# The first group of queries in two parts: an early bound over one key chunk, and sums rescaled afterwards

## The chip, the cores and the metric

The kernel runs on one core of one Trainium2 chip. Five engines work from instruction queues of their own: TensorE (PE, matmuls), VectorE (DVE), ScalarE (ACT, activation functions), GpSimd (POOL) and SyncE (SP, which here only issues DMAs). They meet at semaphores. The metric is the device time of one execution in microseconds, as the median of repeated runs; lower is better.

## The reference

Input x has 2048 tokens of 640 bf16 features. A layer norm gives xn. Two branches read xn, and the output joins them:

```python
x = A_x
xn = _layernorm(x, axis=-1)
s = _A_ref(xn, A_wqkv, A_wo)                       # attention, 32 heads of 20 features
g = _silu(_B_ref(xn, B_w1, B_w2, B_w3, B_w4))      # gated MLP: norm, w1, gelu, shifts, w2, residual, norm, w3, gelu, w4, residual
return x + s * g
```

In the attention, `scores = q @ k.T * Dh**-0.5`, `p = softmax(scores)` over all 2048 keys, `o = p @ v`, and o is projected by wo. 32 heads of 2048 x 2048 scores are 134 million exponentials, which makes the softmax the largest piece of work outside PE.

## The kernel before

**Tiles.** Tokens come in 16 tiles of 128 and 4 chunks of 512. The heads are worked four at a time ("quads", 8 of them), each head on 32 partitions (20 features and a 21st row for the bound). A *group* is one quad and one chunk of 512 queries: 32 groups, named quad_chunk (0_0, 0_1 and so on). For a group and a key tile, a score pair (`score_pair`, two heads, 128 keys x 512 queries each) goes to two PSUM banks; `exp_act` lets ACT take exp of 1024 values per partition into SBUF (line 1604), or, for some tiles named in `BLK` and `UNITS` ("units"), DVE forms the exponential's bits (line 1635, named u...) and pieces of it are shifted by DVE or POOL (lines 1524 and 1522, named s...). `fnpv` (line 1358, named pv...) and line 1536 (named pvd...) multiply by the values and add up in one PSUM bank, PVB. The value matrix has a column of ones, so the sums of the softmax come out with the products. `normalise` transposes the bank (line 1656, named ob...), and divides.

**The bound.** exp needs a shift that is at least roughly the largest score. The kernel takes an upper bound: for each query the sum over features of |q| times the largest |k| of this feature over all keys. In `prep`, `mx_c` reduces |K| of key chunk c (line 1152), `kev_c` copies the keys out on ACT (line 1155, after `mx_c`), `mx_` and `mq_` (lines 1167, 1169) combine the four chunks. `aq_c` takes |q| (line 1129), `sh_c` multiplies it by the bound (four matmuls, line 1136) and `qad_c` adds the result to the queries as their 21st row (line 1142). So no score of group 0_0 can be formed before the keys of all four chunks are projected.

**The opening.** x is loaded in eight DMAs of two tiles (`ld_x0` to `ld_x14`), the weights of the first quad in `ld_wp_1` (keys), `ld_wp_0` (queries), `ld_wv0` (values). The first layer norm is done per tile on DVE (`ln_tiles`: statistics at line 913, norm at line 942, or on POOL at line 938 for tiles in `POOLN`; the power -1/2 on POOL) or on ACT (`ln_tiles_act`: two passes with an accumulator, lines 959 and 961, norm at line 997, or on POOL at line 993). Chunks 0, 1 and 3 are transposed on PE (line 1050, named tr_x) and copied out by ACT (line 1058) or DVE (line 1061), named trev_x; the four tiles of chunk 2 by DMA transposes from SP (tx_8 to tx_11, line 1039). `query(c)`, the key projections KT_c and the value projections v0_n (copied out by vev0_n, line 1296) follow, all through `mm_tile` (line 703). PE also has 36 dummy tasks (`warm`, line 876).

**What sets the order.** The program makes a list of tasks, each with its engine, reads and writes. `TABLE` is a string that lists all of them in one global order, two characters each, with a character for each PSUM or buffer slot; `follow` reads it. Each engine issues its tasks in that order and waits at a task until its operands are there. Nothing is reordered at run time. POOL's tasks and the tasks marked `lock` on DVE are kept apart by waits that `follow` adds.

**Later work.** Groups 0_1 onward need `QM`, a buffer with each head's queries alone on its 32 partitions; POOL zeroes it once (`qm0`, line 1172), and SP copies the queries in (`qm0_1` and so on). The keys and queries of the other quads are projected in "stacks" (s1_0_c is the first, line 1234 copies it out) after SP has loaded `ld_ws0_1`. The MLP branch starts with the loads `ld_w1` and `ld_w2`.

Of the kernel before, what the change touches and what calls it, by code (L numbers as in the profile page):

```python
# [472 lines left out]
class Cfg:  # L473
# [5 lines left out]
    def __init__(self, S=2048, D=640, H=32, F=1536):  # L479
# [20 lines left out]
        self.POOLN = [2, 4, 7, 15]  # L500
# [17 lines left out]
        self.VP0 = False  # L518
# [18 lines left out]
        self.LNA = [3, 2]  # L537
# [36 lines left out]
        self.HP = True  # L574
        self.PP |= {(quad, qc, 0, 2) for quad in range(8) for qc in range(4)}


    def order(self, quad, qc):

        nb = self.ND[quad][qc] % 10
        used = [k for b in self.BLK[:nb] for k in b]
        ks = [k for k in range(self.NT) if k not in used]
        at = {}
        for j, (pos, r, n) in enumerate(self.UNITS[self.ND[quad][qc]]):
            at.setdefault(pos, []).append(("b", j, r, n))
        rows = self.NR[quad][qc]
        out = []
        for i in range(len(ks) + 1):  # L590
            out += at.pop(i, [])
            if i < len(ks):
                out.append(("r" if i in rows else "w" if 100 + i in rows else "k", ks[i]))
        assert not at
        return out
# [22 lines left out]
def c_act(n):  # L618
    return 68 + 0.8333 * n
# [13 lines left out]
class Gen:  # L633
# [149 lines left out]
    def setup_consts(self):  # L783
# [35 lines left out]
        self.free("ones_bf", "ones_f", "m1", "e4", "maskn6")  # L819
# [60 lines left out]
    def xlat(self, n):  # L880
        return 500.0 if n in (2, 4) else 1300.0
# [140 lines left out]
    def ln1_and_transpose(self):  # L1022
# [5 lines left out]
        for g0 in range(0, NT, 8):  # L1028
            na = cfg.LNA[g0 // 8]
            for k0, L in ((0, 2), (2, 2), (4, 4 - na))[:3 if na < 4 else 2]:  # L1030
                tl = list(range(g0 + k0, g0 + k0 + L))
                tmp += self.ln_tiles(f"ln1_{g0 + k0}", tl, lambda n: xn[:, n, :], lambda n: [A("xn", n)], ve_out=True)
            tmp += self.ln_tiles_act(f"ln1a_{g0}", list(range(g0 + 8 - na, g0 + 8)))
# [42 lines left out]
    def prep(self):  # L1076
# [69 lines left out]
        query(0)  # L1146
        for c in range(NQC):
            at = [A("KT", 0, c)]
# [23 lines left out]
        T("pool", 3840, lambda e: e.memset(self.QM[:, :, :, :], 0.0), reads=after, writes=[A("QM", k) for k in range(2)], name="qm0", due=self.at(8))  # L1172
# [4 lines left out]
        shift(0)  # L1177
        for c in range(1, NQC):
            query(c)
            shift(c)  # L1180
# [128 lines left out]
    def attn_quad(self, quad):  # L1309
# [9 lines left out]
        for qc in range(NQC):  # L1319
# [15 lines left out]
            def ends(done=done, total=total):  # L1335
                done[0] += 1
                return done[0] == 1, done[0] == total
            for kind, x, *unit in seq:
                if kind == "k":
# [203 lines left out]
    def score(self, e, out, b, qc, kt, i):  # L1543
        return e.matmul(out, self.KT[32 * i:32 * i + 32, b, 128 * kt:128 * kt + 128], self.QT[32 * i:32 * i + 32, b, 512 * qc:512 * qc + 512],  # L1544
                        start=True, stop=True, tile_position=(32 * i, 0))

    def score_pair(self, b, qc, kt, a, hs, sa, gb):
        T, A = self.T, self.A
        me = []
        def fn(e):  # L1550
            for jj in range(2):
                out = self.bank(hs[jj].slot if isinstance(hs, tuple) else hs.slots[jj])
                if me[0].mode:
                    ins = self.score(e, out[:, :], b, qc, kt, 2 * a + jj)
                    continue
                for c in range(4):
# [4 lines left out]
                    reads=[A("KT", b, kt // 4), A("QT", b, qc), A("QTa", b, qc)] + ([] if gb is None else [A("QM", gb)]),  # L1561
# [80 lines left out]
    def normalise(self, quad, qc):  # L1642
# [9 lines left out]
        else:  # L1652
# [3 lines left out]
        T("dve", c_dve(512), lambda e: e.transpose(Ob[:, :], self.bank(self.PVB)[:, :]),  # L1656
          writes=[("PV", 0), A("Ob")], name=f"ob{quad}_{qc}", cls=cls)
# [191 lines left out]
    def b_alloc1(self):  # L1849
# [9 lines left out]
        vea = [A("VE", n) for g0 in (0, 8) for n in sorted({g0, g0 + 2, g0 + 4, g0 + 8 - cfg.LNA[g0 // 8]})]  # L1859
# [193 lines left out]
    r"#a#9#t$G#,#%#&$R###'7,#8$<#$$$#6$,#:#*#+#;#(#)&J&K$%#-#0#i#.#<$&$'#=#>#`#x#u$($)#v#y#?#w#z$*#@#b#{#_#m#|#j#A#B$-$+#C#D#k#E#n#F$.$/$0%(&#l#G$1#H%-'#I#o"  # L2053
    r"#J#}#K#p#L$3#M#N#d$I#O$K$L#P#f$_$H#q$M$J#h#~#Q$2#R#r$z#$u$#s%#%$p($`%$$q&I$4$5${$|$v$#$k)$l$m$r$w$x$6$N$O#g#c$=#e$>$7$}$s$a$~$?#S$b$n$o$Q$8$;$y$A%D$@$"
    r"B%%$P%&#T%'$C$D$S#U#V$W#W#X$c$E$e#Y#Z#[$t%_#%C%`$d#]$9%f$%g%.$:$F$f%a%b%c&L%%d%2(%/%0%3%4%5%)%*%<)%h$T%i%6$V$U&M$^%+$g$X$Y%1%7#%8$Z%,&b(%=&c%9&N%:&d%;"
    r"%>%?%@&S'%j%k$h&T&U&V$]&O%m#%l&P&e%n$[&W%o%p&f%T$%q%J&%E)&X&Q&g%K$i%L%Y'%Z$j%[%U%]%^%F%G%M%V%N%H%I%O%%P%Q%R%A%S%W%X%B%t(%u%v%r%w%x%{$%y%|%}%e%s%~%z&#&"
    r"$&.%&&&/&'&0&1&7#&8&%&,&&9&:&2#2&-&;&3)~#*$'*#$*+(17*%&4*,)*'#*-$*.(*)*&(&<*(#*6#*2$*3$#^*8&5#*/*0(*1)*5#*7%&=&Z(&[&]'[&^&_&6&o#&p&q&r&(&s&)*P(&`&h*Q&"
    r"*:$*9#&t*4&@#&A*;)*<&B&C*K(*L$*I$&D&E**&i&&j&k&>'&?&l&m*N'*J#&|$&}&~&n*^$*O'*_('#'$*M*U#'%*S'*R*T#&u$&v&w*?&x&y&z''('(')(@'*+%,2(A'+*h&*e(*V$*>*H*f&*i"
    r")'A&'B'C'D'E',*W*Z%*j(*A&F'F'3#'4'&'5'6&G&&H*[#'7'8&{*`$*=*o##5*E*k$*c(*l*a%'-#'.'/'0'1*p''2':(';'<'='>*t#*b'?+'&+)*d)*m('M('@*u$'N'O'P'Q'R*n%*X#'9*Y("
    r"*g++&+-*y(*z&'G('H'I*G+&#'J'K'L*w&+()+5(+7*]'T(*x#'U'V+H#+I('W'X#4*B+J(+9&&a*q'S+K''Y+;'Z*F*{+*#'^('_+S&*r(+U*D+,#*@+^#'`*s%*C*v*|+/&+_&+1(+2$'a(?'b'c"  # L2060
    r"'d&'e'f+.+W(+Y+8%+0%'g(B+:)'h'i+R&+T#+3+4%+[(+<+6$+L'j#'k'l'm+a#+D+V$'n+]'+E+X%+>'p$+`&+'q'r#7+b&,#$,$('o+g''s*}+i't+='u'v+c#+d'+k$']+|'+Z(C(E$+z#+m+e"
    r"+A(F+C,4$+}#(D(G(J,<'+?+{%+F,=&,(#,)'+B+G+o+M'(<+O#,6+N)+P$,8$+~+n+@+j'+l#'w,:'y$(`'z+v,%#'{'|+Q,*$+f'+x.H+s+u'}+t,&%,'+p,3#,+),B$+h$'~+w+r,,,5%-=18,E"
    r"'(#$($,D,F$,]#,G),^(,H+q*~+#+y,-,7',9#(%(&,A$,>#,?$('((,I,C'(H,J()#(*(+,a(,Z#,c,@(,(-&*,k$,;(.,[$,e(,l&,W#,_,X#(/#(0,g,d$(1,f$(2(3,i#(Q,j(,n(,o%,T,Q,K"
    r"(n(R((S(T(U,U#,V)(4(5(=,t&(V,m,p(,M,S,x#,N,v-c&(W,L,Y,z,q&,`((K((L-d',b),|,},w#,s&,u#(M,y((N(O(P,r,P#/,O-+&(o((p,h-,%+$(u'x-$(q(8-.#(r-/),R(6(s,{(t-*-"
    r"?(-3&-4#-0#-%-A(7((9-1$-5&-C(-#-6(,.(g---B#-D%-E-2,~(:(;->&-M(-&-',/,0-@)-O-(-I#,1-)-7-G(-8-J$.](-H#.^-9-Q&-S-P#._.`.a-h(.b-F-L&-R&.J&&Y-i(.K-a%-l(.L-"
    r"N)-b%.M.N-V.P#.Q-`.O(>.R-f$-g)-v#.S-n-w&(I.T-K.U-T.V$.W-o$.6'.7#.X.Y.Z.[-q$-e-p#-k'-m%-U(v$(w-r-j-t$-y#-u(-z)-]-_(x(y(z-Y.8'.'$-W.9'-^-x-{#-s.d-X-Z.e-"
    r"|(-~'.).#$({.I.&#(Y$.c(Z.$$.(%-[.%./.>'-}([.?&.,.:.;$(](^)<(X.f#.g.h(_.i&R.j.*.k.@(.<'.A)2H2R#2J$2L.=.0.l#...m2S#3[2X(2T$2Z2U'.n.o.p2N#2P.22M$2O(.5.4."
    r"B-:-;.32[(2]#2^)2W$.q.-.r#.s2_.1.+.C2I(2Y$2n#.t.u.v.x(2o%2k.y)C2s#2b.D.z2K&.{.|.w2w(3#&2t)2d2V2v#.}.~(h(3$$(i2Q3%&2y2{(2x#(j3,#(k(l2}2`3&'3(&3.&3)(3'3"
    r"*(2c3<#(m)6(3=$3+2e2g3-&2h2z(3;2|'2f2q#)7)83/)92r&2l(323C&(|2i2m(2j2~2u35):3D#2a3>#3?)38)5);3K(312p3F&-<.E3M3H'.F(}((~.G36333A#3G(3J&)`4g3I)#3B%)$)%)&"
    r")J303L&3@3^#3`3](3_)344%&4&$(a((b3:3h(3i(3b#373E3O3f&3d393U3l(3g#4##3Q3N)'(c3a&4$%3c&3P3S3T3n3R3k#3m'3p(41&3V3j3r43#4'/#(d(e/%3o#3q$4((3t4)%)=#)>)?)@)"  # L2070
# [106 lines left out]
```

## Time and profile before

| | |
|---|---|
| median of 3 runs | 806.92 us (805.21 to 808.1) |
| profiled execution, first to last instruction (span) | 799.9 us; the page has no other time for it |
| median run less this span | 7.0 us |
| mean granted TensorE clock | 0.998 |
| busy: PE / ACT / DVE / POOL | 768.0 / 765.4 / 688.9 / 438.8 us |
| first exponential of group 0_0 starts on ACT | 29.84 us |
| the last of the key chunks is copied out by ACT from | 27.66 us |
| first KT/QT matmul on PE | 15.93 us |

Times are from the first instruction of the profiled execution. "Busy" counts the time in which an engine executes; in a timeline a bracket gives the idle time just before the instructions of a line and what released them. Instructions of an engine overlap a little, so the mean length of one (1041 ns for a 1024-wide exponential) is more than the distance between two (40 of them in 36.88 us, 0.92 each).

### The profile page before, as it was taken

The page shows a single profiled execution, that of the slowest core. Times are in us where ns is not written, and L with a number is a line of the kernel's source. Part 1 is how long each engine was busy: PE and PEld are TensorE (multiplying, and loading weights), DVE is VectorE, ACT ScalarE, POOL GpSimd, SP SyncE. Part 2 cuts the span into 40 slices and gives each one's busy share as a digit, 9 for nine tenths or more (in the row PEclk, how much of TensorE's full clock was granted, in tenths as well). Part 3 has the DMA queues.
Part 4 walks back from the last instruction along what each step waited for, and adds up shares of the span by engine and source line. Part 5 has one row for each costly group of instructions (what it writes and reads, how often), then busy time and mean ns, then how long its engine had stood idle before and what let it go on. Part 6 is the DMA issues. An engine that isn't in the chain of part 4 may idle for free.

```text
span 799.9 us, 29391 instructions
## 1 busy us (share of the span) xinstructions
PE 768.0 (96%) x13308; PEld 316.8 (40%) x13308; DVE 688.9 (86%) x908; ACT 765.4 (96%) x797; POOL 438.8 (55%) x232
## 2 busy tenths in 40 slices
PE   7899999999999999999999999999999999998996
PEld 3443333334444433333434444334333444443463
DVE  7868889989999999899988889898878888787767
ACT  7799999999999999999999999999999999999994
POOL 5466556452546647666644655755344454745742
PEclk9999999999999999999999999999999999999999
DMA  6202653243241322524232132314322213115252
GB/s 180 31 14 68 150 145 87 55 117 55 37 86 34 48 68 57 86 54 78 77 100 53 19 82 53 84 36 71 75 63 71 45 37 82 19 28 152 78 151 84
DMA packets 141356, 58.20 MB, mean 73 GB/s; under 512 B 113728, under 2 KB 136432, under 8 KB 141232
## 3 DMA queue, kind: packets, MB, share of 16 engines
q1 hardware_dynamic: 141232, 56.33, 30.9%
q8 instruction: 104, 1.70, 0.9%
q14 instruction: 20, 0.16, 0.1%
HBM read 34.70 MB, written 10.33 MB: 56 GB/s over the span
## 4 chain that ended last, share of the span: by engine, by line
ACT 60%; PE 34%; DVE 4%; DMA 2%; issue 0%; SPq 0%; DVEq 0%
ACT arena L1604 54%; PE psum L703 12%; PE psum L1544 8%; PE psum L1536 5%; PE psum L1358 3%; PE psum L1557 3%; DVE arena L1635 2%; ACT arena L1586 2%; ACT arena L2009 1%; ACT arena L1917 1%; ACT arena L2037 1%; DMA arena<-in_A_x_dram 1%; PE psum L1415 1%; PE psum L1419 1%; DMA arena<-in_B_w_dram 0%; DMA arena<-arena 0%
## 5 line engine op out<-in xcount | busy, mean ns | idle before, releaser
L1604 ACT ACTIVATE arena<-psum 128x1024 bf16<-128x1024 f32 x726 | 677.0, 1041 | 16.1 <-PE psum L1544 11.6
L1522 POOL TENSOR_TENSOR arena<-arena 128x2048 int32<-128x2048 int32 x92 | 330.5, 3600 | 212.2 <-DVE arena L1524 98.7
L1635 DVE TENSOR_SCALAR arena<-psum 128x1024 uint16<-128x1024 f32 x268 | 325.6, 1218 | 51.9 <-PE psum L1544 46.4
L703 PE MATMUL psum<-arena 128*32 128x320 bf16 (+1 forms) x5808 | 329.5, 332 | 2.0 <-DMA arena<-in_B_w_dram 0.7
L1544 PE MATMUL psum<-arena 32*128 32x512 bf16 x1634 | 195.1, 384 | 14.7 <-ACT arena L1604 8.8
L703 PEld LDWEIGHTS psum<-arena 128*32 128x32 bf16 x5808 | 140.9, 96 | 120.8 <-issue 28.8
L1536 PE MATMUL psum<-arena 128*22 128x512 bf16 x2144 | 184.7, 381 | 2.2 <-DVE arena L1524 1.1
L1358 PE MATMUL psum<-arena 128*22 128x512 bf16 x1448 | 137.4, 381 | 0.2
L1524 DVE TENSOR_SCALAR arena<-arena 128x4096 uint16<-128x4096 uint16 (+1 forms) x127 | 133.6, 1075 | 3.4 <-PE psum L1536 2.5
L1544 PEld LDWEIGHTS psum<-arena 32*128 32x128 bf16 x1634 | 53.9, 91 | 183.0 <-ACT arena L1604 101.9
L1557 PE MATMUL psum<-arena 128*32 128x512 bf16 x1400 | 106.7, 381 | 0.1
L1536 PEld LDWEIGHTS psum<-arena 128*22 128x22 bf16 x2144 | 51.3, 91 | 66.8 <-issue 29.9
L1664 POOL TENSOR_TENSOR arena<-arena 128x512 bf16<-128x512 f32 x30 | 41.1, 1369 | 42.3 <-DVE arena L1524 22.3
L1358 PEld LDWEIGHTS psum<-arena 128*22 128x22 bf16 x1448 | 35.6, 91 | 44.3 <-issue 18.9
L1557 PEld LDWEIGHTS psum<-arena 128*32 128x32 bf16 x1400 | 28.5, 95 | 38.8 <-ACT arena L1604 28.7
L2002 DVE CAST arena<-psum 128x512 bf16<-128x512 f32 x48 | 32.8, 684 | 8.0 <-PE psum L703 7.8
L1234 DVE CAST arena<-psum 128x512 bf16<-128x512 f32 x40 | 26.9, 682 | 5.5 <-PE psum L703 5.5
L913 DVE BATCH_NORM_STATS2 arena<-arena 128x6 f32<-128x320 bf16 x54 | 24.6, 481 | 2.8 <-DMA arena<-in_A_x_dram 2.7
L1586 ACT ACTIVATE arena<-psum 128x2048 bf16<-128x2048 f32 x13 | 24.6, 1891 | 1.9 <-PE psum L1544 1.8
L1763 DVE SCALAR_TENSOR_TENSOR arena<-psum,arena 128x320 bf16<-128x320 f32 x32 | 15.4, 486 | 12.4 <-PE psum L703 12.0
L1656 DVE STREAM_TRANSPOSE arena<-psum 128x512 f32<-128x512 f32 x31 | 22.1, 711 | 3.4 <-PE psum L1536 1.6
L1825 POOL TENSOR_TENSOR arena<-arena 128x640 bf16<-128x640 bf16 x12 | 16.8, 1400 | 13.1 <-DMA out_dram<-arena 4.7
(122 smaller groups left out, 335.5 us busy)
## 6 DMA issues: line engine op xcount, KB each, us to landing
arena<-in_B_w_dram SPq DMA_DIRECT2D x48, 160.0 KB, 2.7
arena<-arena SPq DMA_DIRECT2D x124, 32.0 KB, 1.9
arena<-in_B_w_dram SPq DMA_DIRECT2D x4, 960.0 KB, 5.6
arena<-in_A_x_dram SPq DMA_DIRECT2D x8, 320.0 KB, 5.5
arena<-in_A_x_dram SPq DMA_DIRECT2D x16, 160.0 KB, 2.9
out_dram<-arena SPq DMA_DIRECT2D x16, 160.0 KB, 2.3
heads<-arena SPq DMA_DIRECT2D x120, 20.0 KB, 2.0
arena<-keys SPq DMA_DIRECT2D x28, 80.0 KB
```

What stands on the lines that cost most here:

```text
L703: ins = e.matmul(pb[32 * c:32 * c + 32, 0:N], lhsT(k, c), rhs(k, c), start=(k == 0), stop=(stop and k == nk - 1), tile_position=(0, 32 * c))
L1358: ins = e.matmul(pb[32 * i:32 * i + 22, 0:512], VA[:, ql, kts[i // 2], i, :], PT[:, slots[i // 2][0].slot, 512 * (i % 2):512 * (i % 2) + 512],
L1522: return e.tensor_tensor(dst.bitcast(I32), U[:, ub, 0:w].bitcast(I32), bass.AP(c.tensor, c.offset, [list(c.ap[0]), [0, w // 2]]), op=ALU.add)
L1524: fa if onp else lambda e, v=v, dst=dst: e.tensor_scalar(dst, U[:, ub, 0:w], EXP_B[v], None, op0=ALU.add),
L1536: ins = e.matmul(pb[32 * i:32 * i + 22, 0:512], wv, dst[:, at:at + 512].bitcast(BF16), start=first, stop=final, tile_position=(0, 32 * i))
L1544: return e.matmul(out, self.KT[32 * i:32 * i + 32, b, 128 * kt:128 * kt + 128], self.QT[32 * i:32 * i + 32, b, 512 * qc:512 * qc + 512], s ...
L1557: ins = e.matmul(out[32 * c:32 * c + 32, :], self.KT[:, b, 128 * kt + 32 * c:128 * kt + 32 * c + 32], self.QM[:, gb, 2 * a + jj, :], start ...
L1586: lambda e: e.activation(self.PT[:, hp[0].slot:hp[0].slot + 2, :], self.psum[:, 512 * h0.slot:512 * h0.slot + 2048].rearrange("p (a b) -> ...
L1604: lambda e: e.activation(self.PT[:, hp.slot, :], self.psum[:, 512 * hs.slot:512 * hs.slot + 1024], AF.Exp, scale=cfg.scale),
L1635: ins = e.tensor_scalar(U[:, ub, 1024 * at + 512 * k:1024 * at + 512 * k + w], self.psum[:, 512 * hd.slots[k]:512 * hd.slots[k] + w], a_ex ...
L1664: return e.tensor_tensor(OnT.rearrange("p (k d a) -> p a k d", k=4, a=4), Ob[:, :].rearrange("p (a k d) -> p a k d", a=4, k=4), in1, op=AL ...
L2002: T("dve", c_dve(512), lambda e, h=h, fc=fc, i=i, G=G: e.tensor_copy(G[:, i, fc, :], self.wbank(h)[:, 0:512]), reads=[wa], writes=at, name ...
```

## The change

Group 0_0 takes its first four key tiles (0 to 3, key chunk 0; `EARLY = 4`) with other queries than the rest. `early` makes a bound from chunk 0's keys alone (`mqe` from `MXc[0]`, `she` on PE) and adds it to the queries in a buffer of its own (`qade`, into `QE`, which lies in the room of `QM`). Scores of tiles 0 to 3 use `QE`, and their products add up in PVB. When the bound over all keys is known (`qad_0`, as before), `between` forms the difference of the two bounds for every query and head (`fs`: 8 matmuls with the selection matrices `sel`) and ACT takes its exponential (`fe`). `rescale` on DVE multiplies the sums of the first part by it into `Ob`; the bank starts afresh for the other 12 tiles; `sum0_0` adds both parts, and the transpose follows. All four early tiles go through ACT; the group's two units are the key blocks (6, 7) and (10, 11), where they were (2, 3) and (6, 7). `qm0` is moved behind `rescale`, since `QM` holds the early buffers.

```diff
-        self.POOLN = [2, 4, 7, 15]
+        self.POOLN = [6, 8, 9, 14, 15]
-        self.VP0 = False
+        self.VP0 = True
-        self.LNA = [3, 2]
+        self.LNV = [[0], [2, 3], [6, 7], [8, 9], [10, 11], [12, 13]]
+        self.LNS = [[1], [4, 5], [14, 15]]
+        self.EARLY = 4
+        self.PP |= {(0, 0, 1, 3), (0, 0, 1, 2)}
...
+        first = 0 if quad + qc else 1
+        used = [k for b in self.BLK[first:first + nb] for k in b]
...
+            at.setdefault(pos, []).append(("b", j + first, r, n))
...
+        at = at if quad + qc else {k + self.EARLY: v for k, v in at.items()}
...
+        QE = self.QM.rearrange("p a i q -> p (a i q)")
+        self.qe, self.fe = QE[:, 0:512], QE[:, 512:1536].bitcast(FP32)
+        mqe = QE[:, 1536:1664].rearrange("p (j m) -> p j m", m=32)
+        sel = QE[:, 1664:1920].rearrange("p (s j m) -> p s j m", s=2, m=32)
+        def early():
...
+            T("dve", 90, lambda e: e.tensor_scalar(mqe[:, :, 20], self.maskn[:, 0:4], MXc[:, 0:1], None, op0=ALU.mult),
+              reads=[A("MXc", 0), A("maskn"), A("mqe")], writes=[A("mqe")], name="mqe", lock=True)
...
+                for j in range(4):
+                    ins = e.matmul(pb[32 * j:32 * j + 32, 0:512], mqe[:, j, :], self.KS[:, 0:512], start=True, stop=True, tile_position=(0, 32 * j))
...
+            T("dve", c_dve(512),
+              lambda e: e.scalar_tensor_tensor(self.qe, self.wbank(h)[:, 0:512], self.qbias[:, 0:1], QT[:, 0, 0:512], op0=ALU.add, op1=ALU.add),
+              reads=[wa, A("qbias"), A("QT", 0, 0), A("QTa", 0, 0)], writes=[A("QE")], name="qade", rel=h)
+        def between():
...
+                for k in range(2):
+                    for j in range(4):
+                        ins = e.matmul(pb[32 * j:32 * j + 32, 0:512], sel[:, k, j, :], QT[:, 0, 0:512] if k else self.qe, start=k == 0, stop=k == 1,
+                                       tile_position=(0, 32 * j))
...
+            T("act", c_act(512), lambda e: e.activation(self.fe, self.wbank(h)[:, 0:512], AF.Exp, scale=cfg.scale), reads=[wa], writes=[A("FE")],
+              name="fe", rel=h)
         for c in range(NQC):
+            if c == 1:
+                early()
...
-        T("pool", 3840, lambda e: e.memset(self.QM[:, :, :, :], 0.0), reads=after, writes=[A("QM", k) for k in range(2)], name="qm0", due=self.at(8))
...
         shift(0)
+        between()
...
+                if kind == "f":
+                    T("dve", c_dve(512), lambda e: e.tensor_tensor(self.Ob[:, :], self.bank(PVB)[:, :], self.fe, op=ALU.mult), reads=[A("FE")],
+                      writes=[("PV", 0), A("Ob")], name="rescale", cls=-1)
+                    T("pool", 3840, lambda e: e.memset(self.QM[:, :, :, :], 0.0), name="qm0",
+                      writes=[A("QM", k) for k in range(2)] + [A("QE"), A("FE"), A("mqe"), A("sel", 0), A("sel", 1)])
+                    continue
...
+            T("dve", c_dve(512), lambda e: e.tensor_tensor(both, self.bank(self.PVB)[:, :], Ob[:, :], op=ALU.add), reads=[A("Ob")],
+              writes=[("PV", 0), A("On", 0), A("On", 1)], name="sum0_0", cls=cls)
```

The order table is another one throughout. Read off by task names, the opening changes as follows (sx and sxx are the two ACT statistics of a tile, exp a_b with a the key tile and b the pair of heads, shortened):

```
ACT before: sx5 sxx5 sx6 sxx6 sx7 sx14 sxx7 sxx14 sx15 sxx15 trev_x0 x3, norm5 norm6 qev_0 trev_x1 x5, kev_0 norm14
            trev_x3_3 kev_1 kev_2 kev_3 | exp 2_0 0_0 0_1 3_1 1_1 1_0 6_0 ...
ACT after:  sx1 sxx1 sx4 sxx4 norm1 sx5 trev_x0_1 sxx5 trev_x0_4 sx14 trev_x0_2 sxx14 norm5 norm4 kev_0 qev_0 trev_x1 x5,
            sx15 sxx15 | exp 2_1 0_0 1_1 kev_1 exp 2_0 3_0 trev_x3_3 exp 1_0 3_1 kev_2 kev_3 exp 0_1 | 6_0 5_0 fe ...
SP before:  x4 x2 x6 x0 x10 x14 wp_0 wv0 wp_1 x8 x12 | tx_11 tx_10 tx_8 tx_9 ld_ws0_1 qm0_1 qm0_2 ...
SP after:   x0 x2 x4 x6 x8 wp_1 x14 x10 x12 wv0 wp_0 | tx_9 ld_w1 tx_8 tx_10 tx_11 qm0_1 ld_ws0_1 ld_w2 qm0_2 ...
DVE after, from mx_0 on: mx_0 norm7 mqe nb8 (12: rest of the statistics of tiles 10, 11, 13, 12, aq_0 among them) vev0_0 vev0_2 qade
            vev0_1 vev0_3 norm10 norm12 norm11 vev0_7 mx_1 vev0_5 norm13 vev0_6 qev_1 rve, trev_x3 x4, mx_2 ve2 mx_3 mx_ mq_
            vev0_10 aq_1 qad_0 qev_3 u 6 qev_2 u 7 rescale ...
POOL after: ... norm6, norm9, norm8, norm14, norm15, ... r2 qm0 vp0_10 kt0 s0_0_1_3 ... s0_0_1_2 ...
PE after, around the first scores: KT_1 ... sc 2_1 0_0 ... KT_2 ... KT_3, v0_10, sc 0_1 sh_0 ... sc 6_0 ... fs pv k1 ... pv k3 v0_12 ... pv b1
```

Behind the opening, ACT's order is the same from about its 65th to its 270th task but for single exchanges; after that many short stretches differ on all engines.

## The prediction

> **What bounds the kernel now.** First view, busy times and shares of the whole span:
>
> ```profile
> PE 768.0 (96%) x13308; PEld 316.8 (40%) x13308; DVE 688.9 (86%) x908; ACT 765.4 (96%) x797; POOL 438.8 (55%) x232
> ```
>
> ACT and PE are both full to 96%, so I asked where their few idle us lie. Busy time by stretch (columns: stretch and length, then busy us of PE, PEld, DVE, ACT, POOL, then clock, DMA share, GB/s):
>
> ```profile
> 0.00:30.00 30.00, 23.75 (x588) 12.74 (x588) 24.09 (x85) 20.36 (x39) 14.77 (x39) 1.00 0.59 139
> 30.00:60.00 30.00, 28.63 (x500) 12.81 (x500) 22.13 (x34) 29.72 (x33) 17.88 (x16) 1.00 0.05 11
> 60.00:100.00 40.00, 38.77 (x594) 13.43 (x590) 33.73 (x39) 39.63 (x43) 24.90 (x14) 1.00 0.45 109
> 100.00:300.00 200.00, 198.32 (x3322) 79.94 (x3320) 185.00 (x235) 194.06 (x197) 106.08 (x44) 1.00 0.33 73
> 300.00:780.00 480.00, 465.85 (x8008) 190.65 (x8010) 409.14 (x492) 472.09 (x480) 269.77 (x119) 1.00 0.30 69
> ```
>
> ACT idles 9.64 us in the first 30, then 0.28 and 0.37 up to 100. From 100 to 300 PE is the fuller one (1.7 idle in 200), after 300 ACT again (7.9 idle in 480). A lead won on both engines before 37 us therefore has hardly a gap to disappear into. Third view, the chain that ended last, in order of time (start, length, what):
>
> ```profile
> 18.63 2.14 ACT arena L1058 x5
> 20.76 3.69 DMA arena<-arena
> 24.55 3.64 PE psum L703 x64
> 28.60 0.75 DVE arena L1142
> 29.35 0.66 DVE arena L1127
> ```
>
> The chain runs through the DMA transposes of token chunk 2 (they land at 24.46), the key projections of chunks 2 and 3, and qad_0 (28.60), which puts the bound over all keys into the queries. Only then comes the first exponential. ACT's timeline from there back, with the idle time in brackets:
>
> ```profile
> 24.16 0.60 ACT L1058 ACTIVATE arena<-psum 128x512 bf16<-128x512 bf16 x1 [1.27 <-PE psum L1050]
> 25.61 0.78 ACT L1155 ACTIVATE arena<-psum,arena 128x512 bf16<-128x512 f32 x1 [0.86 <-DVE arena L1152]
> 26.59 0.78 ACT L1155 ACTIVATE arena<-psum,arena 128x512 bf16<-128x512 f32 x1 [0.19 <-DVE arena L1152]
> 27.66 0.78 ACT L1155 ACTIVATE arena<-psum,arena 128x512 bf16<-128x512 f32 x1 [0.30 <-DVE arena L1152]
> 29.84 6.52 ACT L1604 ACTIVATE arena<-psum 128x1024 bf16<-128x1024 f32 x7 [1.39 <-PE psum L1544]
> ```
>
> Summed over the timeline, ACT idles 4.5 us before 7.47 (table load, waits for the first tokens) and 5.1 us between 10 and 36.64. The second sum is what exponentials that need key chunk 0 alone could fill.
>
> **The change, part by part.**
>
> *Added work.* ACT: fe, one 512-wide exponential, 0.60 by the 512-wide eviction (L1058, 597 ns). PE: she 4 and fs 8 matmuls; four such take 0.217 us back to back (32 in 1.73), so 0.65. DVE: mqe 0.23 (as L1169), qade, rescale and sum0_0 0.75 each (all read one PSUM and one SBUF operand of 128x512, as L1142, 749 ns): 2.5; the third ACT group adds two small operations (0.3), one norm moves to POOL (0.43 less). POOL: one norm more (0.88), one power (0.7), two sel (0.34 each, as L1304) and a small memset: 2.4, on an engine that idles 15 of the first 30.
>
> *First exponential.* x0 and x2 now load first and are in at about 3.9 and 5.0, where x4 and x2 were; x4 and x6 take the later places (ACT waits for the third load to 7.47, DVE for the fourth to 8.36). DVE's order puts norms 2 and 3 behind three half-tile statistics of x6 and x8 (0.42 each), so chunk 0 is normalised at about 10.6 (now 13.5). The copy-outs of its transposes follow more statistics and end at 14.4; KT_0 starts at 14.5, where QT_0 now starts at 15.93. On ACT, from 7.47: eight statistics at 0.84, three norms at 0.87, eight copy-outs at about 0.46, kev_0 and qev_0 at 0.73: 14.5, so ACT is free at 22.0. On the data side qev_0 ends at 18.5; aq_0 0.28, she 0.39, then qade 0.75, with 2 us of other DVE work between, end at 22.1; a score pair takes 0.39. First exponential: 22.5, against 29.84. wp_0, now the last input load, must be in by 15.8 for QT_0; issued at 10 with 2.5 (shortest weight load) to 6.6 us (median of the pair) to landing, it costs 0 to 0.8, covered by what follows.
>
> *Eight exponentials early.* At ACT's cadence (40 in 36.88: 0.92) they take 7.4; among them stand kev_1, kev_2, kev_3 (0.73 each) and one copy-out (0.5). 22.5 + 7.4 + 2.7 = 32.6. Now the eighth ends at 36.64 + 0.92 = 37.56. If ACT never waited, the lead would be 5.0, less 0.6 for fe: 4.4.
>
> *Second part.* Its first exponential (tile 6) needs qad_0 with the bound over all keys, and DVE has more to do ahead of it: five more value copies (0.43 each, 2.15), qade and mqe 0.98, qev_1 0.75, aq_1 0.28, rve and ve2 0.4, two small ones 0.3, one norm less: 4.4 us. qad_0 ends now at 29.35 with 2.65 us of DVE idle behind it since 3.92: it would end at 31.1 if all this idle went, at 33.8 if none did. I take 33.6, near the upper end, since chunk 2 comes later: its transposes start when norm9, on POOL, is done (about 19.0; now 15.57), and at the same 8.9 us from first issue to last landing they end near 28; KT_2, KT_3 and five value matmul groups (2.9) and sh_0 follow. Then a score pair: exponential of tile 6 at 34.4. Lead over 37.56: 3.1, less fe: 2.5. Bounds of this step: 4.4 (ACT never waits) and 2.3 (33.8). PE can follow: KT_0 starts 1.4 earlier, and of PE's 26.64 us from 10 to 36.64 23.55 are busy, so 3.1 idle to use, against 0.65 of new matmuls.
>
> *rescale, qm0 and what queues there.* rescale needs fe (about 36) and the four early pv; PE's next write to that bank, pv of block 1, is ten steps later, 2.5 us of cover. qm0 (3.51) must now wait for rescale, near 38, and ends at 41.5 (now 38.1). Behind it on POOL are kt0 (1.8) and the two exponent pieces (3.6 each): they end near 52, now at 54.9, so still early. On SP, qm0_1 waits for qm0 with ld_ws0_1, ld_w2 and qm0_2 behind it: ld_ws0_1 goes out at about 44 instead of 26.9 and lands by 49; s1_0_0 on PE (now 57.5) is its first user, 6 us of cover. ld_w1, moved ahead of the transposes, is the second rival.
>
> *Group end.* sum0_0 frees the PV bank in 0.75 where the transpose took 0.72; the transpose after it adds 0.72 on DVE, which idles 7.9 of 30 there. Nothing.
>
> Sum: 2.5 us off. The profiled span is 799.9; the median run is 806.9, so 7.0 lie around it, which I keep: span 797.4, time **804.4** (0.3% is 2.4 us, about what a measurement of this kernel can tell).
>
> **The rivals.**
>
> *Chunk 2 late, gain mostly gone.* ld_w1 (800 KB; such loads take 5.0 us to landing) is issued right after the first transpose. In this trace the four transposes ran with nothing beside them (15.57 to 24.46), so whether a load delays them isn't shown. If they wait for it, the last lands 1.8 to 3.0 later, of which about 1.1 is covered by KT_2's place in PE's order: the lead falls to 0.6 to 1.8, time about 805.7. Against it: from 5 to 10 us the DMAs moved 322 GB/s, at which 800 KB take 2.5 us, so much of the load is gone by the second transpose. The Trainium skill, DMA: Bandwidth & Descriptors, Queues, rings and completion order, has it that each DMA engine takes the descriptors of one issuer's ring in order; by that rule this rival holds, and the time would be 805.7 rather than 804.4.
>
> *Slower: the later order.* The table differs far beyond the opening: same order on ACT from about 65 to 270 us, but many short stretches exchanged after 300. There ACT idles 7.9 and PE 14.2 of 480, so each new wait goes to the end. If ACT's idle there grows by over 4.9, from 7.9 to 12.8, the kernel is slower by 0.3%; if it doubles, the time is 812.3. For it: two full engines leave no slack to hide a bad exchange. Against it: exchanges are between neighbours of equal kind, and can as well remove some of the 7.9.
>
> *All of it works, or more.* ACT never waits at the second part (802.5), or the later order saves 2 us too: about 801.
>
> **How the numbers follow.** Forecast 0.48 (802.5 to 805.2), chunk 2 late 0.24 (within 0.3%, as is the forecast's upper end in small part), slower 0.22, more 0.06. Faster 0.53, same 0.25, slower 0.22. The range reaches from 800.5 (the last case) to 810.0, about half way into the slower one, leaving out nearly 2 in 10. The forecast case's own range is 802.5 to 805.2.
>
> **What would show it.** Right: first exponential near 22.5; seven of L1604 before the last key copy-out (L1155); ACT's idle from 10 us to the ninth exponential down from 5.3 to about 2.5; the ninth starting near 34.4. Wrong: chunk 2's transposes landing after 29.5 and DVE idle ahead of the last maxima; a first exponential after 25 (then statistics or qade are late); ACT idle between 300 and 780 well over 8; or a POOL wait of PE for the pieces of block 1.

## The result, and the profile after

The changed kernel takes 798.88 us (median of 5 executions, 796.28 to 800.78) against 805.96 us (median of 5) for the kernel before: ratio 0.9909, 95% interval 0.9883 to 0.9936. Measured twice more beside other kernels, the ratio was 0.9915 and 0.9921. The forecast of 804.4 had the right sign and about a third of the size, and the time lies below the range of 800.5 to 810.0.

In every execution the time is 1.7 to 1.9 us above its span. The profiled execution after has a span of 797.8 us and took 799.57; the profiled execution of before, with a span of 799.9, therefore took about 801.7 and was 5 us faster than its median. That is the first mistake of the forecast; what lies behind it is taken up with the experiments.

The busy row and the row of granted clocks of the page after:

```profile
PE 774.4 (97%) x13392; PEld 321.2 (40%) x13392; DVE 688.1 (86%) x914; ACT 766.1 (96%) x798; POOL 441.4 (55%) x238
PEclk9999999999999999999999999999999999997998
```

Both bounding engines are as full as before. New is the 7 in slice 37 (718 to 738 us): the clock fell there. In the first profile of before every digit of this row is a 9. Busy time by stretch of the kernel after (columns as in the table of before):

```profile
0.00:30.00 30.00, 25.08 (x626) 15.39 (x630) 23.98 (x88) 22.92 (x41) 17.45 (x50) 1.00 0.70 161
30.00:60.00 30.00, 29.81 (x486) 11.70 (x490) 25.05 (x38) 28.26 (x32) 17.75 (x11) 1.00 0.18 49
60.00:100.00 40.00, 39.82 (x616) 13.70 (x608) 33.43 (x38) 40.00 (x44) 26.53 (x14) 1.00 0.31 78
300.00:780.00 480.00, 470.38 (x8072) 193.74 (x8073) 408.88 (x495) 470.64 (x477) 269.28 (x119) 0.99 0.31 69
```

ACT is busy 2.56 us longer in the first 30 us, gives 1.46 back in the next 30, and idles not at all from 60 to 100. ACT's timeline after (last bracket: idle time and what ended it):

```profile
21.50 2.93 ACT L1654 ACTIVATE arena<-psum 128x1024 bf16<-128x1024 f32 x3
24.32 0.77 ACT L1195 ACTIVATE arena<-psum,arena 128x512 bf16<-128x512 f32 x1
24.99 1.94 ACT L1654 ACTIVATE arena<-psum 128x1024 bf16<-128x1024 f32 x2
27.20 0.60 ACT L1062 ACTIVATE arena<-psum 128x512 bf16<-128x512 bf16 x1 [0.27 <-PE psum L1054]
31.13 1.94 ACT L1654 ACTIVATE arena<-psum 128x1024 bf16<-128x1024 f32 x2 [3.33 <-PE psum L1594]
...
35.92 1.94 ACT L1654 ACTIVATE arena<-psum 128x1024 bf16<-128x1024 f32 x2 [0.60 <-PE psum L1594]
37.78 0.60 ACT L1183 ACTIVATE arena<-psum 128x512 f32<-128x512 f32 x1
```

The first exponential starts at 21.50 (before 29.84; forecast 22.5). Five run, then ACT stands for 3.33 us, and the second part begins at 35.92 (the ninth exponential of before: 37.56; forecast 34.4). The chain that ended last names what ACT waited for:

```profile
23.63 6.26 DMA arena<-arena
29.89 0.04 issue
29.94 0.83 PE psum L708 x12
30.77 0.33 PE psum L1594 x4
31.10 2.74 PE psum L708 x56
```

and the DMA queue of SP shows the cause (last number: how many are issued in that stretch):

```profile
17.68 2.70 SPq L1043 DMA_TRANSPOSE arena<-arena  x1
20.43 0.57 SPq L1937 DMA_DIRECT2D arena<-in_B_w_dram  x1
21.05 4.66 SPq L1043 DMA_TRANSPOSE arena<-arena  x3
```

The last transpose of token chunk 2 is issued by 25.71 and lands at 29.89, 4.2 us later; before, the four were issued by 23.06 and landed at 24.46, 1.4 us later. Between them now goes ld_w1. Behind the landing the keys of chunk 2 (12 matmuls of L708) stand ahead of the next early scores (L1594) in PE's order, and for these ACT waits. So the rival of the late chunk 2 was at work in this execution, and still the kernel is 7 us faster than before. Where do 7 us come from, if this trace leads by only 1.6 us when the opening is over?

To follow a lead through the kernel, I use the start of the first exponential of group 1_0 (quad 1, first query chunk; 123.73 us in the first profile before). Behind it all of them keep this distance to within 0.2 us up to 250 us (g3_twice, which does the same work there, loses 0.3 more by 288). The profiled executions of all kernels below (leads against the first profile of before; "ACT's wait" is the idle time ahead of the sixth exponential, "half clock" the us at granted clock 0.5 between 25 and 50 us):

| kernel | opening | ACT's wait | half clock | lead at 1_0 |
|---|---|---|---|---|
| before, first profile | before | - | 0 | 0 |
| e0_before | before | - | 6.83 | 2.25 behind |
| e2_late | before | - | 0 | 0.44 behind |
| f1_warm, g4_warmlate | before, gaps filled | - | 0, 0 | 0.46, 0.65 ahead |
| changed kernel, a1_after, g2_after | new | 3.33, 2.50, 3.93 | 0, 0, 3.41 | 1.63, 2.09 ahead, 0.10 behind |
| e1_open | new | 0.68 | 0 | 3.74 ahead |
| e3_w1, g1_e3, f3_tail, g3_twice | new, ld_w1 later | 0.68, 0.98, 1.01, 0.86 | 0 in all | 4.06, 3.68, 3.70, 3.42 ahead |
| f2_hold | new, ld_w1 later, early part held | - | 6.83 | 4.64 behind |

One opening, one program, and leads that differ by 2 to 4 us from execution to execution: a single profile could not have told the size.

### The profile page after: what moved, and what is told of

It reads as the page before. It is cut to its first block, busy times and chain, and to the rows that moved or that the text cites. A ratio compares the mean times of both kernels' runs of the same rounds, so it can differ in the third digit from the quotient of the medians.

```text
span 797.8 us, 29573 instructions
## 1 busy us (share of the span) xinstructions
PE 774.4 (97%) x13392; PEld 321.2 (40%) x13392; DVE 688.1 (86%) x914; ACT 766.1 (96%) x798; POOL 441.4 (55%) x238
## 4 chain that ended last, share of the span: by engine, by line
ACT 54%; PE 36%; DVE 5%; DMA 3%; POOL 1%; issue 0%; SPq 0%; DVEq 0%
ACT arena L1654 47%; PE psum L708 13%; PE psum L1594 8%; PE psum L1585 6%; PE psum L1407 4%; PE psum L1607 4%; ACT arena L2065 3%; DVE arena L1685 2%; ACT arena L1636 1%; DMA arena<-arena 1%; ACT arena L1973 1%; ACT arena L2093 1%; DVE arena L1573 1%; PE psum L1464 1%; PE psum L1438 1%; POOL arena L1881 1%
## 5 line engine op out<-in xcount | busy, mean ns | idle before, releaser
L708 PE MATMUL psum<-arena 128*32 128x320 bf16 (+1 forms) x5808 | 336.0, 332 | 1.9 <-DMA arena<-arena 1.2
L1594 PE MATMUL psum<-arena 32*128 32x512 bf16 x1606 | 195.5, 387 | 10.7 <-ACT arena L1654 6.6
L708 PEld LDWEIGHTS psum<-arena 128*32 128x32 bf16 x5808 | 143.2, 96 | 122.0 <-issue 31.5
L1585 PE MATMUL psum<-arena 128*22 128x512 bf16 x2144 | 188.1, 383 | 0.0
L1407 PE MATMUL psum<-arena 128*22 128x512 bf16 x1448 | 137.8, 384 | 0.3
L1594 PEld LDWEIGHTS psum<-arena 32*128 32x128 bf16 x1606 | 53.6, 91 | 177.8 <-ACT arena L1654 97.7
L1607 PE MATMUL psum<-arena 128*32 128x512 bf16 x1512 | 114.9, 381 | 0.3
L1607 PEld LDWEIGHTS psum<-arena 128*32 128x32 bf16 x1512 | 31.6, 95 | 40.9 <-ACT arena L1654 30.2
```

The source lines that it names most:

```text
L708: ins = e.matmul(pb[32 * c:32 * c + 32, 0:N], lhsT(k, c), rhs(k, c), start=(k == 0), stop=(stop and k == nk - 1), tile_position=(0, 32 * c))
L1407: ins = e.matmul(pb[32 * i:32 * i + 22, 0:512], VA[:, ql, kts[i // 2], i, :], PT[:, slots[i // 2][0].slot, 512 * (i % 2):512 * (i % 2) + 512],
L1585: ins = e.matmul(pb[32 * i:32 * i + 22, 0:512], wv, dst[:, at:at + 512].bitcast(BF16), start=first, stop=final, tile_position=(0, 32 * i))
L1607: ins = e.matmul(out[32 * c:32 * c + 32, :], self.KT[:, b, 128 * kt + 32 * c:128 * kt + 32 * c + 32], self.QM[:, gb, 2 * a + jj, :], start ...
```

## The experiments

Three explanations were open: the opening gains more than I gave it; the later order, which I had counted at nothing, gains; or the kernel before loses something that its first profile does not show. The runs come in three sets, one for each first letter (a1_after belongs to f), the first on one chip and the other two on another, each with the kernel before among them. Kernels of different sets are compared by their ratios to it.

**e0_before: the kernel before once more.** No edit.

> The kernel before, unchanged, beside itself on this chip. The two profiles differ by 2.1 us of span (799.9 and 797.8), the medians by 7.1 us (805.96 and 798.88), and the profiled run of the changed kernel took 799.57, only 1.8 more than its span. Theory A: the first profile of the kernel before is a fair one; then its runs here have spans of 799 to 801 and times of 801 to 803. Rival B: its typical run is longer than that profile; then spans are 802 to 806 here, at the same 1.8 us around them, and its new trace shows the extra us in some stretch that the old trace lacks. Ratio to the kernel before 1.000 in both.

Measured: 805.14 us (median of 12), ratio 1.0011 (0.9991 to 1.0032). Its span is 803.9 us and its time 1.8 more, as rival B has it, and its profile shows what the first lacked. Busy time by stretch:

```profile
30.00:35.00 5.00, 3.98 (x26) 0.91 (x26) 4.85 (x7) 4.10 (x5) 0.77 (x1) 0.65 0.01 3
35.00:40.00 5.00, 5.00 (x72) 2.04 (x68) 2.12 (x3) 3.24 (x4) 4.79 (x3) 0.66 0.05 15
```

The clock is granted at half for 6.83 us from 31.5 on, ACT starves behind PE (3.24 busy of 5), and the execution is 2.25 us behind at group 1_0. A second stretch of 10.24 us at half clock begins at 724.4 and costs 2.25 more (1.82 behind at 690 us, 4.07 at the end). Over the 37 executions of before in this set, time goes with the mean clock: turned into us at half clock, (1 - mean clock) x 2 x span, the line through them is 800.9 us + 0.24 per us at half clock (correlation 0.84), with a median of 19 us at half clock. The first profile had 3.3, all of it in its last 3.3 us: by this line it is 3.8 us faster than the median, of the 5 to be explained. In the two later sets the line has a slope of 0.21 (23 executions, correlation 0.86) and of 0.08 (11 executions, 0.31), so the price of a us at half clock is not one number.

**e1_open and e2_late: the change in two halves.** The order table is cut at one place (about 285 us) where both kernels stand at the same state.

```diff
 e1_open: the changed kernel's code
+TABLE = after[:2265] + before[2250:]
 e2_late: the code of the kernel before
+TABLE = before[:2250] + after[2265:]
```

> The changed kernel's opening (two-part first group, its prologue, its order up to about 285 us) with the old order from there on. In the two traces the exponentials of groups 1_0 to 2_3 start 1.44 to 1.64 us earlier in the changed kernel. Theory A, the opening alone gives its lead of 1.4 and no more: 1.4 us under the kernel before, ratio 0.998. Rival B, the opening gives most of the 7.1 us because it changes something that lasts: 5 us or more, ratio 0.994 or less.

> The kernel before with its own opening and the changed kernel's order from about 285 us on. In the two traces the lead grows from 1.44 at 288 us to 3.47 at 690 us, so by theory A the later order gives 2.0 us, less what the last 60 us take back (the lead at the end is 2.1): ratio 0.998 to 1.000. Rival B, the later order is the larger part of the 7.1 us: 4 to 6 us, ratio 0.993 to 0.995.

Measured: the opening alone 800.81 us, ratio 0.9944 (0.9923 to 0.9965); the later order alone 801.76 us, ratio 0.9967 (0.9950 to 0.9983). The product, 0.9911, is the whole change. So the opening brings 4.5 us (2.8 to 6.2), the later order 2.7 (1.4 to 4.0). Neither size that I had named came out in either run: 4.5 lies between 1.4 and 5, 2.7 between 2 and 4. For the later order the traces agree with no need of the clock: e2_late is 0.44 us behind the first profile of before at 288 us and 1.57 ahead at 668, with ACT idle 2.97 and 1.24 us in the stretches in which before has 3.81 and 2.26 (289 to 501 and 501 to 669 us). That is 2.0 us against the first profile, and 1.2 to 1.7 against e0_before, f1_warm (below) and e1_open, which have the old order there and gain 0.4, 0.4 and 0.8 on that profile themselves. The rest of the later order's gain is in the tail: from 668 us to the end e0_before loses 2.25 against the first profile and e2_late 0.8, both with 10.24 us at half clock.

**e3_w1: ld_w1 behind the transposes.**

```diff
 SP: tx_9
-    ld_w1
     tx_8 tx_10 tx_11
+    ld_w1
```

> The changed kernel with one entry of the order table moved: ld_w1 (800 KB) is issued after the last DMA transpose of chunk 2 instead of after the first. In the changed kernel's trace the four transposes are issued from 17.68 to 25.71 and chunk 2 lands at 29.89, 4.2 us after the last issue ends; before, without a load among them, it was 1.4 us. Theory A, the load holds them up: chunk 2 lands at 26.5 to 27.2, ACT's wait of 3.33 us before the sixth exponential falls to under 1.2, and the exponentials of group 1_0 start 1.5 to 2.5 us earlier than in the changed kernel. Rival B, the transposes are late because their tokens are normalised late or their issues are slow: landing after 29, no gain.

Measured: 796.56 us, ratio 0.9891 (0.9867 to 0.9916). It was run again beside the changed kernel itself:

> The changed kernel with the load of w1 issued behind the four transposes of the second key chunk, a second time and now on the same chip as the changed kernel itself. Theory (the second key chunk is held up behind that load in some executions of the changed kernel, by about 2 us, and never with the late load): 1 to 2 us faster than the changed kernel beside it, its slowest execution faster than the changed kernel's slowest by 2 us or more, and no idle time over 1 us on ScalarE ahead of the exponentials near 29 us. Rival (the load only changes where the time is lost): within 0.5 us of the changed kernel.

> The changed kernel unchanged, beside the late load of w1 and the two others. 797 to 799.5 us on both theories; with the first theory of the late load its profiled execution has, as two of the three before, the second key chunk landing about 30 us and ScalarE idle for over 2 us ahead of it.

g1_e3 took 796.82 us (795.68 to 797.68; ratio 0.9901), the changed kernel beside it 799.94 us (795.20 to 802.55; 0.9921). The changed kernel came out 0.4 above the range that I had given it. Over all executions of both, from all sets, 11 with the late load lie between 794.8 and 797.7 and 16 without between 795.2 and 802.6; the ratio of their means is 0.9973 (0.9957 to 0.9990). SP's queue and the chain of g1_e3:

```profile
17.93 7.93 SPq L1043 DMA_TRANSPOSE arena<-arena  x4
25.91 0.58 SPq L1937 DMA_DIRECT2D arena<-in_B_w_dram  x1
```

```profile
24.58 3.26 DMA arena<-arena
```

The chunk lands at 27.84 although its issues end at 25.86, and ACT's wait is 0.98 us. In g2_after it lands at 30.05, PE and ACT run dry, and the clock falls. The landing in the chain of g2_after, ACT's timeline, and its busy time by stretch:

```profile
23.95 6.10 DMA arena<-arena
```

```profile
31.88 1.94 ACT L1654 ACTIVATE arena<-psum 128x1024 bf16<-128x1024 f32 x2 [3.93 <-PE psum L1594]
```

```profile
26.00:30.00 4.00, 1.78 (x80) 1.12 (x72) 2.25 (x6) 1.68 (x3) 2.26 (x7) 1.00 0.94 95
30.00:32.00 2.00, 1.90 (x20) 0.47 (x24) 0.12 (x1) 0.12 (x1) 0.00 (x0) 0.61 0.00 0
```

That execution has nothing left of its opening's lead. So the rival is right as a mechanism, a wait of 2.5 to 3.9 us in three of the four profiled executions with the load in between. The fourth, e1_open with 0.68, is no exception to the order of the queue. In all four the second transpose, next behind the load, lands 2.0 to 2.1 us after the load does (changed kernel: load 26.05, transpose 28.15; a1_after 25.71 and 27.67; g2_after 26.15 and 28.29; e1_open 24.29 and 26.35). In e1_open the load was issued at 19.04, in the others at 19.32 to 20.63, and landed 1.4 to 1.9 us sooner; the last transpose then lands at 27.51, as in the kernels with the late load (27.47 to 28.11). The wait takes about half of the opening's lead in two executions and, with the clock, all of it in g2_after; over all executions, by the ratio above, it is worth 2.1 us, so it does not take most of the gain.

**a1_after: the changed kernel, beside the next three.**

> The changed kernel unchanged, on the same chip as the others of this call, so that they can be set beside it directly. Both theories: median 797 to 800 us, mean granted clock of its executions about 0.991 to 0.992.

797.61 us, ratio 0.9915 (0.9891 to 0.9938).

**f1_warm: the gaps of before filled.** Six more groups of matmuls on zeros, and warm35 moved up ahead of them; nothing else.

```diff
-        self.NPF = [36, 0]
+        self.NPF = [36, 6]
 PE: sc 2_0 2_1
+    warm35
     sc 0_0
+    warmer0 warmer1
     sc 3_0 0_1
+    warmer2
     sc 3_1
+    warmer3 warmer4
     sc 6_1 1_1
-    warm35
+    warmer5
```

> The kernel before, with six more groups of four matmuls on zeros in the four gaps that TensorE has between 29.8 and 32.7 us (0.26, 0.46, 0.25 and 0.41 us), and nothing else changed. Theory (part of what the new opening brings is clock: in most executions of the kernel before the granted clock falls to half for some 7 us right behind these gaps, as in its second profiled execution from 31.5 to 38.4 us): the clock stays at 1.0 between 30 and 40 us, the mean clock of its executions rises from about 0.988 to about 0.991, and the time falls by 1 to 2.5 us (ratio 0.997 to 0.9988). Rival (the opening gains only by its earlier exponentials, and the first profiled execution before was fast for another reason): time within 0.5 us of the kernel before, or slower by the added matmuls, at most 0.5 us, and the same mean clock.

Measured: 802.32 us (median of 12), ratio 0.9965 (0.9946 to 0.9984): 2.8 us for matmuls on zeros. Its busy time by stretch, to be set beside that of e0_before:

```profile
30.00:35.00 5.00, 4.96 (x60) 1.45 (x60) 4.98 (x8) 5.00 (x6) 0.30 (x1) 1.00 0.01 3
35.00:40.00 5.00, 5.00 (x104) 2.54 (x96) 3.46 (x6) 4.72 (x6) 5.00 (x3) 1.00 0.03 8
```

PE has no gap left, the clock stays, ACT is full. The theory is confirmed in kind; in size it explains part. The mean of its executions has 12.0 us at half clock where before beside it has 15.4; 3.4 us at 0.21 to 0.33 each (the line of this set, and e0_before's 2.25 for 6.83) are 0.7 to 1.1 us. Another 0.4 to 0.7 us is a stall of PE near 75 us, put down to "issue" (the profile shows nothing that PE waited for) in all three profiles of before's opening and absent in f1_warm and g4_warmlate; why the added matmuls remove it is not known. The sum, 1.1 to 1.8, reaches only the lower end of the interval (1.3 to 4.3); the rest of the 2.8 is not accounted for.

**g4_warmlate: both gains that need no two-part group.** f1_warm up to about 285 us, the changed kernel's order behind.

```diff
+TABLE = f1_warm[:2256] + after[2265:]
```

> The kernel before with the six groups of matmuls on zeros in the gaps of TensorE at 30 to 33 us, and behind 285 us the order of the changed kernel: both gains that have nothing to do with the two-part first group. If they add, its ratio to the kernel before is 0.9965 x 0.9967 = 0.9932, 799.3 to 800.5 us, and the changed kernel beside it is another 1.5 to 2.5 us faster, which is what the two-part group and its prologue bring by themselves. Rival (the opening's 4.5 us are the two-part group's own, and the matmuls on zeros gain the same thing only by chance): the changed kernel is 4 us or more faster than this one.

Measured: 799.64 us, ratio 0.9940 (0.9924 to 0.9956), as the product says. The changed kernel beside it is at 0.9921, with the late load at 0.9901. So what the two-part group and its prologue bring beyond the filled gaps is the difference of two ratios: 0.0019 or about 1.5 us as the change has it (with both intervals, from 4 us gained to 1 lost, so it is not shown to be more than nothing), and 0.0039 or about 3.1 us (1.3 to 5) when chunk 2 is not held up.

**f2_hold: the early start alone undone.** Late load as in e3_w1; prologue, first bound and rescaling stay, the eight early score pairs and exponentials go behind the key copies.

```diff
 ACT: ln1a_14_sxx15
-     exp 2_1 0_0 1_1
      kev_1
-     exp 2_0 3_0
      trev_x3_3
-     exp 1_0 3_1
      kev_2 kev_3
+     exp 2_1 0_0 1_1 2_0 3_0 1_0 3_1
      exp 0_1 6_0 ...
 PE:  their score pairs and pv k2 likewise, behind the keys of chunk 3
```

> The changed kernel with the late load of w1, and with the first part's eight score pairs, exponentials and its attention matmul held back until the last key chunk is copied (behind kev_3); the new prologue, the bound over the first chunk and the rescaling stay. It undoes the early start alone. Theory (the early start is what the opening gives): ScalarE stands idle from about 24 to 32 us but for the key copies, the eight exponentials of 0.97 us come behind it, and the lead of the opening is gone: 6 to 8 us slower than with the early start, 802 to 805 us, that is about level with the kernel before. Rival (the new prologue, by bringing the keys earlier, gives the gain, and the early exponentials only fill time): at most 3 us slower than with the early start, below 800 us.

Measured: 806.52 us, ratio 1.0016 (0.9999 to 1.0033), some 10 us behind e3_w1. ACT's timeline:

```profile
32.66 7.66 ACT L1654 ACTIVATE arena<-psum 128x1024 bf16<-128x1024 f32 x8 [1.55 <-PE psum L1594]
41.02 1.02 ACT L1654 ACTIVATE arena<-psum 128x1024 bf16<-128x1024 f32 x1 [0.70 <-PE psum L1594]
```

The second part begins at 41.02 instead of 33.51, 7.5 us later, nearly the eight exponentials' 7.66. The 2 to 3 us beyond the expected 6 to 8 go with a half clock of 6.83 us that begins at 36.8, after PE was busy 1.27 and 0.51 us of 2 from 32 to 34 and 34 to 36. Within the new opening the early start is the gain; the new prologue without it gains nothing. The 10 us are not what the two-part group is worth against before, whose first exponential starts at 29.84, where this kernel's starts at 32.66.

**f3_tail: the tail of before in e3_w1.**

```diff
+TABLE = e3_w1[:4765] + before[4750:]
```

> The changed kernel with the late load of w1, and behind table entry 4765 (about 660 us) the order of the kernel before. In the profiled executions the new order leads by 2 us up to 690 us and gives back up to 4 of its lead in the last two groups, where the granted clock was halved for 10.2 us from about 720 us. Theory A (what is given back is the clock's doing, which falls behind gaps of TensorE that both orders have there): within 1 us of the late load of w1 alone (796.6 us). Theory B (the new order of the tail costs 2 us or more itself): 793.5 to 795 us.

Measured: 798.94 us, ratio 0.9930 (0.9905 to 0.9954). Both theories fell: the old tail is 2 to 3 us slower than the new one. In its profiled execution, the slowest of the six, the lead goes from 5.44 us at 668 to 0.28 at the end, with 10.24 us at half clock from 716.6 and 3.41 more from 767.8; e3_w1, with the same first stretch, goes from 5.99 to 5.23. With the 1.2 to 2.0 us of the order ahead of the tail this comes to 3 to 5 us for the whole later order, where e2_late has 2.7 (1.4 to 4.0), so how the gain divides between the two is not settled. What looked in the traces like a lead given back by the new tail was a comparison of tasks whose places had changed.

**g3_twice: the gaps in the tail filled.** Nine score pairs of group 7_1 are computed twice into the same bank, so the result is the same.

```diff
+TWICE = {("7_1", k, a) for k, a in ((11, 0), (1, 0), (10, 0), (0, 0), (10, 1), (6, 0), (15, 0), (5, 1), (1, 1))}
...
-                    ins = self.score(e, out, ...)
+                    for _ in range(2 if (self_tag, kt, a) in TWICE else 1):
+                        ins = self.score(e, out, ...)
```

> The kernel with the late load of w1, in which nine of the score pairs of group 7_1 (712 to 720 us) are computed twice over into the same bank, about 2.5 us of added matmuls in a stretch in which TensorE idles 2.3 us in seven gaps. Theory (the granted clock is halved behind such a run of gaps, and the halved clock costs about 1 us there): no stretch at half clock between 715 and 735 us, mean granted clock of its executions from 0.992 to 0.996 or more, time 0.5 to 1.5 us below that with the late load beside it. Rival (the halved clock there comes from the load on the chip, not from gaps): the mean clock stays at 0.992 and the time is the same or up to 1 us longer.

Measured: 794.78 us (794.03 to 795.24), ratio 0.9877 (0.9861 to 0.9893), 2.0 us below g1_e3 beside it and a little more than the 0.5 to 1.5 expected. Every one of its executions has a mean clock of 0.998, where g1_e3 has 0.992 in the median, so the rival, a clock that falls with the load on the chip, is out. Busy time by stretch, g1_e3:

```profile
712.00:722.00 10.00, 7.87 (x70) 1.75 (x62) 7.50 (x7) 9.55 (x11) 5.66 (x3) 0.75 0.50 130
722.00:735.00 13.00, 12.73 (x232) 5.49 (x228) 9.43 (x11) 12.17 (x12) 5.53 (x4) 0.93 0.39 114
```

and g3_twice:

```profile
712.00:722.00 10.00, 8.37 (x104) 2.50 (x100) 8.00 (x8) 9.88 (x11) 4.91 (x3) 1.00 0.52 130
722.00:735.00 13.00, 12.35 (x244) 5.79 (x244) 9.78 (x12) 12.86 (x14) 6.82 (x4) 1.00 0.40 125
```

Half a us more of PE work in ten keeps the clock, and ACT gains 1.0 us of busy time in the 23. This is the fastest kernel of the study, ahead of the changed kernel by 3 to 5 us.

## Why the prediction was wrong in size

*The base.* "so 7.0 lie around it, which I keep" is the first step that failed. 1.8 us lie around a span; the other 5 were that the profiled execution was a fast one, most of it (3.8 by the line of the first set) because it kept its clock and the median execution does not. By itself this doesn't move the forecast, which is the median less 2.5 with either base. But it hid a cost of the kernel before inside a number that I took to lie outside the kernel, so I read the gain of the opening from a trace whose opening loses nothing to the clock.

The Trainium skill, TensorE: Matmul & The Clock Gate, Part 1, has a clock that falls to half after an idle window of about 3.4 us, counted in windows that run free of the program. The lengths agree: the stretches here, 3.41, 6.83, 10.24 and 13.65 us, are one to four such windows, and the same gaps trigger in one execution and not in the next. The idle window doesn't: no gap ahead of these stretches in before is longer than 0.46 us near 30 us (1.4 us in all) or 1.07 us near 720. The same page of the Trainium skill, in A second HAM failure mode: psum-queue depth-cycling, has a kernel whose clock oscillates because PE idles briefly and often between groups of matmuls. That is nearer to what these runs show.

*Added work* held for ACT (766.1 us against 765.4, forecast 0.6 more) and POOL (2.6 us more, forecast 2.4). DVE was put too high: e1_open, which has the opening alone, has 690.0 against 688.9, 1.1 more where I had about 2.4. The 84 more matmuls belong to the later order: e1_open has 13308, as before.

*First exponential*: 22.5 forecast, 21.50 to 22.19 measured. Right, slightly too late; the terms listed after 18.5 add up to 21.9, not 22.1.

*Eight exponentials early*: the start was right; "if ACT never waited" held in no execution. The wait ahead of the sixth is 0.68 to 1.01 us at best.

*Second part*: 34.4 forecast with a lead of 3.1. Measured 33.5 to 34.1 where chunk 2 is on time and 35.5 to 37.7 where it is not. At group 1_0, fe paid, the leads are 3.4 to 4.1 and from 2.1 down to -0.1; the forecast's 2.5 lies between them. The term was sized about right for the mechanism, but I gave one number to two cases that alternate. The sum also gives 0.8 us to the step from qad_0 to the exponential, priced at 0.39; it took 0.49 before (29.35 to 29.84) and 0.64 after. The sign that I had named, ACT's idle time from 10 us to the ninth exponential falling from 5.3 to 2.5, is 4.75 in the profile after and 2.53 in e3_w1.

*rescale, qm0 and what queues there*: rescale came at 39.49 and qm0 from 40.23 to 43.74 (forecast 38 to 41.5), ld_ws0_1 at 47.16 (44). The cover held: PE had one gap over 0.15 us between 30 and 60, of 0.19.

*Group end*: nothing, as forecast, since the lead from there on is unchanged.

*Chunk 2 late* (0.24): the mechanism is shown, by the move of ld_w1. My argument against it, that most of the load would be gone by the second transpose, failed in all four profiled executions: that transpose never landed before the load. The page of the Trainium skill that I had named, DMA: Bandwidth & Descriptors, has one issuer's ring taken in order by each engine. All four agree with it, with the second transpose 2.0 to 2.1 us behind the load; whether the last transpose is late then hangs on when the load lands, 24.29 or about 26. Both signs of this rival stood in the profile after: the last transpose at 29.89, and DVE idle 1.77 us ahead of a maximum over the keys.

*The later order*, which the sum has at nothing, is the second step that failed: it gains 2.7 us. "Slower" (0.22) had the sign wrong, and "the later order saves 2 us too" had 0.06. The table behind 285 us takes ACT's idle time from 6.1 to 4.2 us between 289 and 669, and it loses less in the tail. The sign that I had named for slower, ACT idle "well over 8" between 300 and 780, did come (9.4), but behind 712, where the clock falls and where the earlier end moves into the window. I had looked at how many stretches differ and not at what ended the idle time in each of before's.

In sum, forecast 2.5. Shown by halves: opening 4.5, later order 2.7. So besides the base two terms of the sum failed: the later order, put at nothing without a reason from the trace, and the opening's 2.5, which was set against a trace of before that loses less in its opening than a common one. By the profiled executions the new opening leads the first profile by 1.8 us in the mean of four, and the other two executions with before's opening are 0.4 and 2.25 behind it; that brings the opening's gain to 2 to 4 us, so part of the 4.5 is not located. g4_warmlate shows that about 3 of the 4.5 can be had without the two-part group, by filling gaps of before's opening; of these the clock is shown, the stall at 75 us is seen but not explained, and the rest is open.

## What to carry to other kernels

Compare the profiled execution's own time with the median before anything is summed: if it is faster, ask what it was spared, and look at the clock row of a second profile. Where PE idles in several short gaps one after the other, ahead of a stretch in which another engine lives off PE, filling the gaps (even by computing a score twice) can be worth as much as a change of the algorithm: 2.8 us and 2.0 us here, where the two-part group brings some 1.5 to 3 beyond the filled gaps. And a load put between transposes that someone waits for should go behind them, even if it is harmless in some executions.

## What the runs showed of the hardware

- In each of the fourteen profiled executions all changes of the granted clock lie a whole number of windows of 3.41 us apart, and where the first lies differs from execution to execution. In the window just ahead of each of the 31 falls PE was idle for 0.94 to 2.69 us, in one gap (1.55 us in f3_tail, 2.0 near the end of before) or in several of 0.2 to 1.4. Of 22 windows at full clock with over 1.4 us idle the clock fell behind 19; of 28 with 0.94 to 1.4 it fell behind 12; behind none with less. It came back only behind windows with at most 0.2 us idle. So where the windows fall upon the gaps matters, but it doesn't decide alone: windows with 0.97 us idle lie near 30 us in before, e2_late and e0_before, and only in e0_before did the clock fall.
- What half clock costs differs: from 668 us to the end the old tail lost 1.8 and 2.25 us against the first profile with 10.24 us at half clock (f1_warm, e0_before) and 5.2 with 13.65 (f3_tail). The new tail lost 0.8 to 1.4 with 10.24, but g3_twice, at full clock up to 790 us, gains 1.75 there, so half clock costs the new tail about 2.5 to 3 as well. In the opening 6.83 us cost e0_before 2.25.
- The last of the transposes lands 1.4 to 2.6 us after the end of its issue with no load ahead of it in the queue, and 4.1 to 4.2 with an 800 KB load that lands at about 26 us. With the same load landing at 24.29 it was 2.2 (e1_open).
